# Per-head transposes straight from the loaded q and k runs, and a reordered first slot, in an attention-plus-feed-forward kernel on one Trainium2 core

## The chip, the cores and the metric

The kernel runs on one NeuronCore of one Trainium2 chip, as one launch. The metric is device time in microseconds (us); lower is better. The kernel before takes 341.52 us, the median of 4 runs (340.52 to 342.38).

## The reference

Eight batches of eight heads, 576 tokens, head size 64, everything in fp32. Each head does causal attention in a window of 128 tokens with a linear distance bias; its output, laid out as 4608 tokens by 512 features, goes through a two-layer feed-forward block.

```python
scores = scale * np.matmul(q, k.transpose(0, 1, 3, 2))
bias = slopes[:, None, None] * (-np.abs(rel).astype(np.float32))[None, :, :]
mask = (rel >= 0) & (rel < window)                      # window = 128
attn = softmax(np.where(mask, scores + bias[None], -1e9))
x = np.matmul(attn, v).transpose(0, 2, 1, 3).reshape(B * S, H * D)
h = x @ w_in                                            # 512 -> 2048
out = (h * np.clip(h + 3.0, 0.0, 6.0) / 6.0) @ w_out    # 2048 -> 512
```

## The kernel before

The attention works on pairs of heads. One pair of one batch is a step g, counted from 0 to 31: batch b = g // 4, pair hp = g % 4. Each step needs q and k with the head size on the partitions (`qTb`, `kTb`) and v with the tokens on the partitions (`vbuf`), all in bf16.

There are two ways in for q and k. Batches 0 to 2 take the first: `load_runs` puts six consecutive tokens on each of 96 partitions ("runs"), mostly by POOL's DMA queue, which casts to bf16 on the way. `prepare` (L206) copies a pair's runs into a small tile `pr`, in an order in which one [96, 128] block holds both heads of every sixth token. `transposes` (L222) turns six such blocks per tensor on PE, and `settle` (L239) copies the result from PSUM into `qTb` or `kTb`. Batches 3 to 7 take the second: `load_tokens` fetches five pieces of 128 tokens on SP's queue (L121), `cast_tokens` casts them into the single tile `tbuf` on POOL (L196), and `xbar` (L201) transposes by DMA. All loads land in four buffers, `ldbuf0` to `ldbuf3`: the runs of batches 0, 1 and 2 in `ldbuf0`, `ldbuf2` and `ldbuf0`, the first pair of batch 0 in `ldbuf3` ("wide", fp32), the token loads where `slot_of` says.

Every engine runs its instructions in the order of the program text. `first_batch` emits steps 0 to 3 and the beginning of 4, `segment` the rest. A step g emits its scores (L259 to L277), the transposes of step g + 1, the exponentials on ACT (L288, L291, L301, L309, L312), masks on POOL (`affine_select`, L294 and L304), the product with v of step g - 1 (L333, L336), the transposes of the result into `xT` (L362), `prepare(g + 2)` and then `stage_next(g)`, which issues the next loads and casts.

The feed-forward block is cut into units of four matmuls. `fill(n)` emits n units at a place in the text: an up unit `hps` (L375, followed by ACT L379 and DVE L380), or a down unit `ops` (L407). From step 9 on each step holds eight units. A finished output tile is copied to `osb` (L413, L415) and its store (L417) goes out on ACT's queue ahead of the next unit. Transfers on SP's and ACT's queues share eight completion semaphores handed round among them, so a transfer's issue also waits for the earlier transfer that used its semaphore.

Of the kernel before, what the change touches and what calls it, by code (L numbers as in the profile page):

```python
# [11 lines left out]
BF16 = mybir.dt.bfloat16  # L12
# [6 lines left out]
def kernel(  # L19
# [9 lines left out]
    nc = tc.nc  # L29
    B, H, S, D = q.shape  # L30
# [5 lines left out]
    NP = H // 2  # L36
    NQ = 5
# [3 lines left out]
    RP, RT = 96, 6  # L41
# [14 lines left out]
    ident = perm.tile([128, 128], BF16)  # L56
# [6 lines left out]
    bias_o = perm.tile([128, H], FP32)  # L63

    held = ctx.enter_context(tc.tile_pool(name="held", bufs=1))
    prs = ctx.enter_context(tc.tile_pool(name="prs", bufs=2))
    ppool = ctx.enter_context(tc.tile_pool(name="ppool", bufs=2))
    small = ctx.enter_context(tc.tile_pool(name="small", bufs=2))
    gpool = ctx.enter_context(tc.tile_pool(name="gpool", bufs=2))
# [18 lines left out]
    def slot_of(b, nm):  # L88
        if b < 3:
            return (1, 3, 1)[b]  # L90
        return (3, 1, 0, 2)[(3 * (b - 3) + "qkv".index(nm)) % 4]

    runs = {}
    for b in range(NB_PE):
        t = ldbuf[(0, 2, 0)[b]][:, :].bitcast(BF16)
        for n, nm in enumerate("qk"):
            runs[b, nm] = t[:RP, ts(n, H * RT * D)].rearrange("p (h c) -> p h c", h=H)
    wide = {nm: ldbuf[3][:RP, ts(n, 2 * RT * D)].rearrange("p (h c) -> p h c", h=2)
            for n, nm in enumerate("qk")}

    def load_runs(b, nm, hs, dst, eng):
        eng.dma_start(out=dst,
                      in_=src_of[nm][b, hs, :, :].rearrange("h (p t) d -> p h (t d)", t=RT))

    def load_pairs(b, nm, lo, hi):
        hs = slice(2 * lo, 2 * hi)
        load_runs(b, nm, hs, runs[b, nm][:, hs, :], nc.gpsimd)
# [18 lines left out]
    def constants():  # L126
        nc.vector.memset(bias3, 0.5)
        nc.vector.memset(warm, 0.0)
        nc.scalar.activation(out=warm, in_=warm, func=ACT.Exp)
        make_identity(nc, ident)  # L130
        for nm in "qk":
            load_pairs(0, nm, 1, 2)
        nc.gpsimd.iota(rel_i, pattern=[[0, 1]], base=0, channel_multiplier=1)
        base = rpool.tile([128, NT], FP32, tag="r6", name="base")
        base_i, base_b = base[:, 0:128].bitcast(INT32), base[:, 256:320].bitcast(BF16)
        nc.gpsimd.iota(base_i, pattern=[[0, 128]], base=-64, channel_multiplier=1)
        nc.gpsimd.tensor_copy(out=base_b, in_=base_i)
        nc.gpsimd.affine_select(out=base_b, in_=base_b, pattern=[[1, 128]],
                                channel_multiplier=-1, base=0,
                                compare_op=ALU.is_ge, fill=-(2.0 ** 30))  # L140
        nc.gpsimd.memset(p4buf[1], 1.0)
        nc.gpsimd.memset(kTb[1][:, :, 4, LAST:128], 0.0)
        nc.gpsimd.memset(vbuf[1][:, :, :, D:W], 1.0)
        nc.gpsimd.memset(vbuf[1][64:128, 4, :, 0:D], 0.0)
        for hp in range(2, NP):
            for nm in "qk":
                load_pairs(0, nm, hp, hp + 1)
        for nm in "qk":
            load_pairs(1, nm, 0, 2)
        nc.vector.memset(kTb[0][:, :, 4, LAST:128], 0.0)  # L150
        nc.vector.memset(vbuf[0][:, :, :, D:W], 1.0)
        nc.vector.memset(vbuf[0][64:128, 4, :, 0:D], 0.0)
        nc.vector.memset(p4buf[0], 1.0)
        for h in range(H):
            nc.vector.tensor_scalar(out=tab[:, h, :], in0=base_b, scalar1=slopes[h] / scale,
                                    scalar2=0.0, op0=ALU.mult, op1=ALU.add)
# [12 lines left out]
    def load_w_in(g):  # L169
        nc.gpsimd.dma_start(  # L170
            out=w_in_sb[:, :, ts(g, 512)],
            in_=moe_w_in[:, ts(g, 512)].rearrange("(k p) f -> p k f", p=128))
# [6 lines left out]
    def cast_v(b, j, eng):  # L179
        n = min(128, S - j * 128)  # L180
        copy = nc.scalar.copy if eng is nc.scalar else eng.tensor_copy
        copy(out=vbuf[b % 2][:n, j, :, 0:D], in_=ld[b, "v"][:n, j, :, :])
# [21 lines left out]
    st = {}  # L204

    def prepare(g):  # L206
        b, hp = divmod(g, NP)
        hs = slice(2 * hp, 2 * hp + 2)
        for nm in "qk":
            pr = prs.tile([RP, RT, 2, D], BF16, tag=f"pr{nm}", name="pr")  # L210
            if (g == 0 and nm == "k") or (nm == "q" and NP <= g < NP + 2):
                copy = nc.scalar.copy
            elif (nm == "q" and g < NP) or g == 1:
                copy = nc.vector.tensor_copy
            else:
                copy = nc.gpsimd.tensor_copy
            src = wide[nm] if g == 0 else runs[b, nm][:, hs, :]
            copy(out=pr.rearrange("p t e d -> p e t d"),  # L218
                 in_=src.rearrange("p e (t d) -> p e t d", t=RT))
            st[g, nm] = pr  # L220

    def transposes(g):  # L222
        b, hp = divmod(g, NP)
        if g > 2 * NP:
            pair = ps_sc.tile([128, 2, 512], FP32, tag="sc", name="tpp")
        tps = {}
        for nm in "qk":
            src = st.pop((g, nm)).rearrange("p t e d -> p t (e d)")
            if g > 2 * NP:
                tp = pair[:, "qk".index(nm), 0:S // 2].bitcast(BF16).rearrange(  # L230
                    "p (t a) -> p t a", t=RT)
            else:
                tp = ps_h.tile([128, RT, RP], BF16, tag="h", name="tp", padded_shape=[128, 8, 128])
            for t in range(RT):
                nc.tensor.transpose(tp[:, t, :], src[:, t, :], ident[:RP, :RP])  # L235
            tps[nm] = tp
        st[g, "tps"] = tps

# [202 lines left out]
    def stage_next(g):  # L441
        b, hp = divmod(g, NP)
        if g == 0:
            load_w_in(0)
        if g == 1:
            load_pairs(1, "q", 2, NP)
            load_pairs(1, "k", 2, NP)
        if g in (2, 3):
            load_w_in(g - 1)
        if g in (4, 5):  # L450
            load_pairs(2, "q", 2 * (g - 4), 2 * (g - 3))
            load_pairs(2, "k", 2 * (g - 4), 2 * (g - 3))
        if g == 4:
            load_w_in(3)
        if g == 5:
            load_tokens(2, "v")
        if g == 6:
            load_w_out(0)
            load_w_out(1)
            load_tokens(3, "q")  # L460
        if g in (7, 8):
            load_w_out(g - 5)
        if g == 7:
            cast_tokens(2, "v")
            load_tokens(3, "k")
        if g == 8:
            cast_tokens(3, "q")
        if g == 9:
            load_tokens(3, "v")
            xbar(3, "q")  # L470
            cast_tokens(3, "k")
        if g == 10:
            xbar(3, "k")
            load_tokens(4, "q")
        if g == 11:
            cast_tokens(3, "v")
            load_tokens(4, "k")
            load_tokens(4, "v")
            cast_tokens(4, "q")
        if b >= 3 and b + 1 < B:  # L480
            if hp < 2:
                xbar(b + 1, "qk"[hp])
            if hp in (0, 2):
                cast_tokens(b + 1, "kkv"[hp])
        if b >= 3 and b + 2 < B:
            if hp > 0:
                load_tokens(b + 2, "qkv"[hp - 1])
            if hp == 3:
                cast_tokens(b + 2, "q")
# [6 lines left out]

    def first_batch():
        transposes(0)
        settle(0)
        biases()  # L500
        prepare(1)
        for g in range(NP):
            scores(g)
            exp_diag(g, 0)
            spin(0)
            transposes(g + 1)
            settle(g + 1)
            exp_off(g, 0)
            exp_off(g, 1)
            if g == 0:  # L510
                for j in range(NQ):
                    cast_v(0, j, nc.scalar if j < 3 else nc.gpsimd)
            prepare(g + 2)
            if g == 1:
                spin(0)
            if g > 0:
                values(g - 1, (0, 1, 2))
                values(g - 1, (3, 4))
            if g > 1:
                back(g - 2)  # L520
            if g == 2:
                more_constants()
            stage_next(g)
        g = NP
        scores(g)
        back(g - 2)
        values(g - 1, (0, 1, 2))
        values(g - 1, (3, 4))
        exp_diag(g, 0)
        for j in range(3):  # L530
            cast_v(1, j, nc.gpsimd)
        exp_off(g, 0)
        exp_off(g, 1)
        transposes(g + 1)
        settle(g + 1)
        back(g - 1)
        done[0] = g
        prepare(g + 2)
        cast_v(1, 3, nc.gpsimd)
        cast_v(1, 4, nc.gpsimd)  # L540
        fill(1)
        stage_next(g)
        fill(1)

# [97 lines left out]
```

## Time and profile before

| | |
|---|---|
| median of the runs | 341.52 us (340.52 to 342.38) |
| the profiled execution's own time | 342.38 us |
| its span in the trace | 340.7 us |
| busy: PE, DVE, ACT, POOL | 316.5, 175.7, 199.0, 151.6 us |
| DMA | 48.14 MB, mean 141 GB/s over the span |
| L218 `pr` copies | 16 on POOL, 5 on DVE, 3 on ACT |
| L235 transposes | 144 of 96x96, 0.20 to 0.28 us each, pipelined |

The span is what the trace covers; 1.7 us of the execution's own time lie outside it. Busy time of PE is modelled from pipelined matmuls, so a busy PE is not one at its peak. An engine's idle time costs something only where the chain of waits passes through it. Times of day below are microseconds from the start of the span. The scores of steps 0 to 4 begin at 7.8, 12.5, 20.8, 24.4 and 27.6 us, those of step 10 at 69.0 and of step 14 at 107.4.

### The profile page before, as it was taken

To read this page: it belongs to the slowest core of one execution; us is meant where nothing else is said; L and a number is where in the kernel's file an instruction comes from. 1 tells how busy PE (TensorE), PEld (TensorE's weight loads), DVE (VectorE), ACT (ScalarE), POOL (GpSimd) and SP (SyncE) were. 2 spreads that over 40 slices of the span, in tenths; PEclk is the share of its full clock that TensorE was granted. 3 is DMA by queue.
4 is the path that set the end of the run, shared out by engine and by line. 5 is a ranking of instruction groups with operands and counts; after the bars stand their busy time and mean duration, and the time that the engine had idled before them with its cause. 6 is when DMAs were issued, how large, how long until landed. Compare 5 with 4: busy or idle time off the path is not lost.

```text
span 340.7 us, 6827 instructions
## 1 busy us (share of the span) xinstructions
PE 316.5 (93%) x2615; PEld 164.1 (48%) x2615; DVE 175.7 (52%) x362; ACT 199.0 (58%) x350; POOL 151.6 (45%) x261
## 2 busy tenths in 40 slices
PE   6488998989989999999999999999999999999995
PEld 5365655444444444545454444554455444444443
DVE  5477887646354445455545555545555444444410
ACT  3748776665457475767576757675765344343401
POOL 8389869356824763666366726632331000000000
PEclk9569999999999999999999999999999999999999
DMA  9999999999999999699959994510111000100021
GB/s 177 209 207 208 201 207 210 184 211 193 220 214 173 216 205 204 145 212 206 240 112 201 224 245 88 96 50 33 54 50 52 31 31 31 63 31 31 33 92 62
DMA packets 134831, 48.14 MB, mean 141 GB/s; under 512 B 121360, under 2 KB 130320, under 8 KB 134800
## 3 DMA queue, kind: packets, MB, share of 16 engines
q1 hardware_dynamic: 122464, 33.89, 54.8%
q0 software_dynamic: 8672, 7.44, 14.1%
q10 hardware_dynamic: 3664, 6.39, 5.4%
q8 instruction: 20, 0.33, 0.5%
q14 instruction: 11, 0.09, 0.1%
HBM read 36.70 MB, written 9.44 MB: 135 GB/s over the span
## 4 chain that ended last, share of the span: by engine, by line
PE 64%; DMA 10%; ACT 8%; DVE 6%; SPq 4%; POOL 4%; issue 4%; ACTq 0%; POOLq 0%
PE hps L375 28%; PE ops L407 27%; DMA ldbuf<-in_q_dram 5%; DMA ldbuf<-in_v_dram 4%; SPq L121 3%; DVE g L380 3%; ACT r L379 3%; ACT po L301 2%; ACT pd L291 2%; POOL pd L294 2%; DMA ldbuf<-in_k_dram 2%; PE av L336 1%; PE scd L271 1%; SPq L201 1%; PE av L333 1%
## 5 line engine op out<-in xcount | busy, mean ns | idle before, releaser
L380 DVE SCALAR_TENSOR_TENSOR g<-r,hps 128x512 bf16<-128x512 f32 x144 | 98.9, 687 | 132.0 <-ACT r L379 132.0
L379 ACT ACTIVATE r<-hps,bias 128x512 f32<-128x512 f32 x144 | 99.6, 692 | 109.2 <-PE hps L375 102.3
L375 PE MATMUL hps<-xT,w_in_sb 128*128 128x512 bf16 x576 | 146.9, 379 | 5.7 <-DVE g L380 5.5
L407 PE MATMUL ops<-w_out_sb,g 128*128 128x512 bf16 x560 | 141.8, 379 | 0.0
L407 PEld LDWEIGHTS <-g 128*128 128x128 bf16 x560 | 54.3, 98 | 63.5
L375 PEld LDWEIGHTS <-w_in_sb 128*128 128x128 bf16 x576 | 50.8, 97 | 58.7 <-issue 8.8
L304 POOL TENSOR_SCALAR_AFFINE_SELECT po<-po 128x512 bf16<-128x512 bf16 x64 | 40.1, 638 | 22.2 <-ACT po L301 19.6
L294 POOL TENSOR_SCALAR_AFFINE_SELECT pd<-pd 128x512 bf16<-128x512 bf16 x46 | 28.1, 636 | 41.0 <-ACT pd L291 41.0
L196 POOL CAST tbuf<-ldbuf 128x512 bf16<-128x512 f32 (+1 forms) x50 | 28.8, 615 | 37.2 <-issue 21.9
L301 ACT ACTIVATE po<-sco,bias_o 128x512 bf16<-128x512 f32 x64 | 43.2, 691 | 0.0
L342 DVE TENSOR_TENSOR avs<-av,rc 128x384 bf16<-128x384 f32 (+1 forms) x56 | 28.0, 500 | 1.9
L291 ACT ACTIVATE pd<-scd,bias_d 128x512 bf16<-128x512 f32 x46 | 29.0, 685 | 0.0
L336 PEld LDWEIGHTS <-pd 128*128 128x128 bf16 x256 | 19.0, 98 | 10.3 <-POOL pd L294 1.2
L333 PE MATMUL av<-vbuf,po 128*128 128x65 bf16 x224 | 21.3, 194 | 1.6 <-DVE avs L342 0.8
L336 PE MATMUL av<-vbuf,pd 128*128 128x65 bf16 x240 | 21.8, 195 | 0.6 <-POOL pd L294 0.6
L333 PEld LDWEIGHTS <-po 128*128 128x128 bf16 x256 | 19.0, 99 | 5.0 <-DVE avs L342 1.3
L413 ACT COPY osb<-ops 128x512 f32<-128x512 f32 x18 | 10.6, 586 | 12.8 <-PE ops L407 12.8
L235 PE MATMUL tp<-ident,pr 96*128 96x96 bf16 x108 | 8.4, 226 | 7.9 <-POOL pr L218 4.2
L312 ACT ACTIVATE p4buf<-sco,bias_d 128x64 bf16<-128x64 f32 x46 | 15.0, 326 | 0.0
L415 DVE COPY osb<-ops 128x512 f32<-128x512 f32 x17 | 11.6, 684 | 5.8 <-PE ops L407 5.8
L288 ACT ACTIVATE pd<-scd 128x1024 bf16<-128x1024 f32 x9 | 9.3, 1031 | 8.3 <-PE scd L271 8.3
L235 PEld LDWEIGHTS <-pr 96*128 96x128 bf16 x144 | 7.9, 105 | 12.2 <-POOL pr L218 4.4
(75 smaller groups left out, 228.0 us busy)
## 6 DMA issues: line engine op xcount, KB each, us to landing
ldbuf<-in_v_dram SPq DMA_DIRECT2D x32, 256.0 KB, 5.4
out_dram<-osb ACTq DMA_DIRECT2D x23, 256.0 KB, 3.5
ldbuf<-in_q_dram SPq DMA_DIRECT2D x20, 256.0 KB, 5.3
ldbuf<-in_k_dram SPq DMA_DIRECT2D x20, 256.0 KB, 5.5
out_dram<-osb SPq DMA_DIRECT2D x12, 256.0 KB, 2.0
w_in_sb<-in_moe_w_in_dram POOLq DMA_DIRECT2D x4, 512.0 KB, 9.0
w_out_sb<-in_moe_w_out_dram POOLq DMA_DIRECT2D x4, 512.0 KB, 8.7
ldbuf<-in_q_dram POOLq DMA_DIRECT2D x4, 288.0 KB, 8.4
```

The lines of the kernel that those rows point to most:

```text
L196: nc.gpsimd.tensor_copy(out=tbuf[:m, :, j, :], in_=s[:m, j, :, :].rearrange("p (i e) d -> p i (e d)", e=2))
L291: nc.scalar.activation(out=pd[:, e, :, :].rearrange("p j c -> p (j c)"), in_=sc[:, e, :], func=ACT.Exp, bias=bias_d[:, h:h + 1], scale=scale)
L294: nc.gpsimd.affine_select(out=pd[:, e, :, :], in_=pd[:, e, :, :], pattern=[[0, 4], [1, 128]], channel_multiplier=-1, base=0, compare_op=AL ...
L301: nc.scalar.activation(out=po[:, e, :, :].rearrange("p j c -> p (j c)"), in_=sc[:, e, :], func=ACT.Exp, bias=bias_o[:, h:h + 1], scale=scale)
L304: nc.gpsimd.affine_select(out=po[:, e, :, :], in_=po[:, e, :, :], pattern=[[0, 4], [-1, 128]], channel_multiplier=1, base=-1, compare_op=A ...
L333: nc.tensor.matmul(av[:, i, e, :], lhsT=po[:, e, qt - 1, :], rhs=vb[:, qt - 1, h, :], start=True, stop=False)
L336: nc.tensor.matmul(av[:, i, e, :], lhsT=d, rhs=vb[:, qt, h, :], start=(qt == 0), stop=True)
L342: nc.vector.tensor_tensor(out=st[g, "avs"][:, qts[0]:qts[0] + nq, :, :], in0=av[:, 0:nq, :, 0:D], in1=rc[:, 0:nq, :, :].to_broadcast([128, ...
L375: nc.tensor.matmul(hps, lhsT=w_in_sb[:, ks, ts(ms, 128)], rhs=xT[:, ks, ts(nt, NT)], start=(ks == 0), stop=(ks == n_ks - 1))
L379: nc.scalar.activation(out=r6, in_=hps, func=ACT.Relu, bias=bias3[:, 0:1], scale=1.0 / 6.0)
L380: nc.vector.scalar_tensor_tensor(out=gts[nt][:, ms, :], in0=r6, scalar=1.0, in1=hps, op0=ALU.min, op1=ALU.mult)
L407: nc.tensor.matmul(ops[nt, sub], lhsT=gts[nt][:, ms, ts(sub, 128)], rhs=w_out_sb[:, ms, :], start=(ms == 0), stop=(ms == n_ms - 1))
```

## The change

The reordering copy disappears for every step but the first. `transposes` takes the [96, 64] block of one head and one token position directly from the loaded runs and writes it to the half of the output partitions that belongs to that head, so there are twice as many transposes, each with half the columns. Step 0 still casts its fp32 runs, now in the order in which they were loaded. The pool `prs` has one buffer in place of two.

POOL issues the runs of pairs 2 and 3 of batch 0 before its memsets. The first runs of batch 1 are issued in `stage_next(0)`, ahead of the first part of w_in. The casts of batch 0's v come after `stage_next(0)` in the text. In `slot_of` two buffers change places: v of batch 3 goes to `ldbuf2` and q of batch 4 to `ldbuf0`, and so on in the same rotation.

```diff
-    prs = ctx.enter_context(tc.tile_pool(name="prs", bufs=2))
+    prs = ctx.enter_context(tc.tile_pool(name="prs", bufs=1))
...
-        return (3, 1, 0, 2)[(3 * (b - 3) + "qkv".index(nm)) % 4]
+        return (3, 1, 2, 0)[(3 * (b - 3) + "qkv".index(nm)) % 4]
...
+        for hp in range(2, NP):
+            for nm in "qk":
+                load_pairs(0, nm, hp, hp + 1)
         nc.gpsimd.memset(p4buf[1], 1.0)
         nc.gpsimd.memset(kTb[1][:, :, 4, LAST:128], 0.0)
         nc.gpsimd.memset(vbuf[1][:, :, :, D:W], 1.0)
         nc.gpsimd.memset(vbuf[1][64:128, 4, :, 0:D], 0.0)
-        for hp in range(2, NP):
-            for nm in "qk":
-                load_pairs(0, nm, hp, hp + 1)
-        for nm in "qk":
-            load_pairs(1, nm, 0, 2)
...
         for nm in "qk":
-            pr = prs.tile([RP, RT, 2, D], BF16, tag=f"pr{nm}", name="pr")
-            if (g == 0 and nm == "k") or (nm == "q" and NP <= g < NP + 2):
-                copy = nc.scalar.copy
-            elif (nm == "q" and g < NP) or g == 1:
-                copy = nc.vector.tensor_copy
-            else:
-                copy = nc.gpsimd.tensor_copy
-            src = wide[nm] if g == 0 else runs[b, nm][:, hs, :]
-            copy(out=pr.rearrange("p t e d -> p e t d"),
-                 in_=src.rearrange("p e (t d) -> p e t d", t=RT))
+            if g > 0:
+                st[g, nm] = runs[b, nm][:, hs, :]
+                continue
+            pr = prs.tile([RP, 2, RT * D], BF16, tag=f"pr{nm}", name="pr")
+            copy = nc.scalar.copy if nm == "k" else nc.vector.tensor_copy
+            copy(out=pr, in_=wide[nm])
             st[g, nm] = pr
...
-            src = st.pop((g, nm)).rearrange("p t e d -> p t (e d)")
+            src = st.pop((g, nm))
...
             for t in range(RT):
-                nc.tensor.transpose(tp[:, t, :], src[:, t, :], ident[:RP, :RP])
+                for e in range(2):
+                    nc.tensor.transpose(tp[e * D:(e + 1) * D, t, :], src[:, e, ts(t, D)],
+                                        ident[:RP, :RP])
...
         if g == 0:
+            load_pairs(1, "q", 0, 2)
+            load_pairs(1, "k", 0, 2)
             load_w_in(0)
...
-            if g == 0:
-                for j in range(NQ):
-                    cast_v(0, j, nc.scalar if j < 3 else nc.gpsimd)
             prepare(g + 2)
...
             stage_next(g)
+            if g == 0:
+                for j in range(NQ):
+                    cast_v(0, j, nc.scalar if j < 3 else nc.gpsimd)
```

## The prediction

> **What bounds the kernel now.** I read the page's slices first, then the chain of waits in order of time, then the timeline at the places where the chain leaves PE.
>
> ```profile
> PE   6488998989989999999999999999999999999995
> PEclk9569999999999999999999999999999999999999
> DMA  9999999999999999699959994510111000100021
> ```
>
> A slice is 8.5 us. From the 14th on (about 112 us) PE is full to the end: nothing there is late, and none of it is touched by the change. So the change can only move the time at which PE gets there. The DMA row is full from the start to beyond that point. That is the second resource to watch.
>
> The timeline shows the largest hole at 14 us.
>
> ```profile
> 13.50 0.61 POOL L182 CAST vbuf<-ldbuf 128x512 bf16<-128x512 f32 x1 [2.16 <-DMA ldbuf<-in_v_dram]
> 16.82 0.61 POOL L182 CAST vbuf<-ldbuf 64x512 bf16<-64x512 f32 x1 [2.71 <-DMA ldbuf<-in_v_dram]
> 17.38 0.82 POOL L218 COPY pr<-ldbuf 96x768 bf16<-96x768 bf16 x1
> ...
> 18.26 0.66 PE L235 MATMUL tp<-ident,pr 96*128 96x96 bf16 x6 [4.18 <-POOL pr L218]
> ```
>
> The bracket is the idle time before the row and what ended it. PE stands for 4.18 us for a copy that POOL could have made at 13.2 us, when the k run had landed (issued 5.96, 7.2 to landing), but POOL was held by two v casts whose pieces had not come.
>
> Between 31 and 48 us the chain goes round a loop of 6.7 us per step, on DVE as much as on PE:
>
> ```profile
> 38.31 1.90 PE hps L375 x8
> ...
> 40.96 0.69 DVE g L380
> ...
> 41.64 0.76 DVE qTb L244
> 42.40 0.66 DVE kTb L244
> ```
>
> No copy that the change removes is in this loop. Further on the chain runs through transfers:
>
> ```profile
> 65.90 5.22 DMA ldbuf<-in_k_dram
> ...
> 71.20 0.37 ACTq L417
> ...
> 71.68 0.10 ACT r L379
> ...
> 72.26 1.27 ACT pd L291 x2
> ...
> 73.57 0.67 PE tpp L235 x12
> ```
>
> The first store, on ACT's queue, is issued only when a k transfer of batch 3 has landed at 71.1: it reads no k, but shares its completion semaphore. ACT stood 1.96 us, and PE then 0.93 us for `pd`. The same happens at 91.6 us with a q transfer, and the last such place is here:
>
> ```profile
> 98.54 4.57 SPq L201
> ...
> 103.15 3.94 DMA ldbuf<-in_v_dram
> ...
> 109.39 1.18 POOL pd L294 x2
> ...
> 111.80 0.20 PE av L333
> ```
>
> POOL had waited 9.7 us for a DMA transpose, and PE found its mask just in time at 111.8.
>
> **What the Trainium skill says.** "TensorEngine Tiling", Performance Considerations: stationary operands of at most 64 columns can be packed two abreast; Restrictions: column tiling switches Fast Weight Load off. No row of this trace has 64 stationary columns; the nearest, the scores on half the rows, come at 28 ns each (8 in 0.39 us, the last 0.20), against 60 ns for the blocks of 128 columns in L362 (5 in 0.44). "TensorE: Matmul & The Clock Gate", Part 3: weight loads overlap running matmuls only for different row groups; the two heads here share theirs. Its section LDWEIGHTS prices a load at columns / 1.2 ns, 53 ns for 64. "DMA: Bandwidth & Descriptors", Queues, rings and completion order: all queues take turns on the same 16 engines. The trace agrees: while POOL's queue is full a 256 KB piece on SP's takes 13 to 22 us to land, against a median of 5.4.
>
> **The change, part by part.**
>
> *Copies.* POOL loses 16 x 0.821 = 13.1 us, DVE four (3.1 us with one of 1.50), ACT two (1.7 us). On the path are those of the first 28 us; afterwards POOL's idle time covers them (1.6 to 2.5 us before its masks at 42.8 and 49.5), and DVE and ACT lose none after step 5. The two casts of step 0 stay; a plain order instead of a permuted one I take at zero (0.72 and 0.83 us now, at best half).
>
> *The hole.* Transposes(2) can start at 13.4 and be settled at about 15.0. The product of step 0 then needs the last v piece, landed at 16.6 now. With 0.59 MB of batch 1 out of the queue, at about 210 GB/s, it lands 2.8 us sooner; POOL, after masks until 11.35 and three DMA issues of 0.68 to 0.76 us, is at the casts at 13.5 and done by 14.7. Scores(2) at 15.2 instead of 20.8; if v lands as now, 17.5.
>
> *Batch 1's first runs.* Issued at 7.8 and 8.5 now, 11.4 and 12.1 after, so k lands at 12.1 plus 9.4 (a later pair's time; bounds 8.0 and 11.8) = 21.5. The k transposes of step 4, at 25.3 now, wait for that: of 5.6 us gained **3.8** remain (1.4 to 5.2). w_in, issued 5 us sooner, is needed at 31. The four POOL memsets slip 2.5 us behind four DMA issues; p4buf's first reader is at 15.2. prs with one buffer is used once: nothing.
>
> *Twice the transposes.* 144 more, all before 75 us. The spacing now is (0.67 - 0.206)/11 = 42 ns. Call the new one s. Two abreast would be 23 ns, one after the other 42, bound by the weight load 53, load and matmul in turn 95. I take **53**. In the loop of steps 4 to 7, DVE wants q at 41.64, 0.46 us after the transposes begin: q is late by 12s - 0.26 = 0.38 us, k by less. Four times makes 1.5. Steps 9 and 10 add 24s - 0.51 = 0.76 us on PE each, 1.5. So 3.0 of the 3.8 go, and PE comes **0.8 us early** to the store at 70 us. With 23 or 42 ns it is 3 to 4 us early.
>
> *Slots.* The runs in ldbuf2 are last read by transposes(7), near 42 us, v comes at 72; those in ldbuf0 by transposes(11), 74.2, q at 82.9. SP's queue holds k and v of batch 4 behind that load, so a slip beyond 8 us would delay them; none is in sight. Nothing.
>
> *The queue.* Here I decide. When the k transfer lands is a matter of the bytes before it: v of three batches, three batches of runs, both weights, q of batch 3, some 13 MB at about 200 GB/s. None goes away; they only change order. POOL's transfers go out 3 to 4 us sooner, take turns with SP's as before and end sooner; the k transfer ends where the sum ends. What can be won is a dip:
>
> ```profile
> 16.00:18.00 2.00, 0.00 (x0) 0.00 (x0) 0.00 (x0) 0.00 (x0) 1.18 (x2) 0.50 1.27 234
> 18.00:20.00 2.00, 1.74 (x25) 1.60 (x26) 1.04 (x2) 0.00 (x0) 1.99 (x4) 0.50 0.83 180
> ```
>
> (The two last columns are DMA share and GB/s.) With w_in and the runs queued by then it fills: 2 x (1.25 - 0.83)/1.25 = **0.7 us**. Bounds: 0, as the pieces may only be reordered, and 2 us if the dips at 37 and 60 us fill too. After 72 us the SP chain (transposes through the single `tbuf`, L201) keeps its own pace, so 0.7 us is what reaches 111.8.
>
> Sum: 342.38 - 0.7 = 341.7 for the profiled execution, which lies 0.86 above the median; against the median 341.52 - 0.7 = **340.8 us**.
>
> **Rivals.** Half a percent, 1.7 us, is about what a measurement can tell here.
>
> *A: the queue takes it back* (above). For it: the chain enters transfers three times between 51 and 112 us, ACT already waits at the store. Against: the DMA row is not quite full near 60 and 75 us. 339.8 to 342.2. Also here: the early part doing nothing at all, since any gain is dropped at the store.
>
> *B: the head's gain goes through.* Then the k transfer was late because its predecessors were issued late, not because the wires were full. Speaks for it: SP issued one q piece at 51.4 that landed 11.4 us later, and single issues took up to 6 us. With 23 or 42 ns a transpose worth 2.5 to 4 us: 337.5 to 339.0.
>
> *C: slower.* The place is the loop and steps 9 and 10: heads share row groups, so each weight load waits for the transpose before it, s = 95 ns. Then k is late by 24s + 0.16 - 1.14 = 1.3 us in each of four steps, and steps 9 and 10 pay 1.77 each: 8.7 us against 3.8 gained and 1.9 of ACT's slack, 3.0 us late. 344.5. It decides from s = 74 ns on, where 144s - 4.9 = 5.7. For it: the skill's two sentences on weight loads. Against: loads of 128 columns hide behind 42 ns now.
>
> **How the numbers follow.** A 0.44, B 0.31, C 0.25. The predicted time is A's, 340.8. The tails of A across 339.8 are put against those of B across it, so faster 0.32, same 0.43, slower 0.25. The range leaves out the best of B and the worst of C: 337.8 to 344.5.
>
> **What would show it.** L218 left with two rows, POOL's busy time near 138 us. PE's wait at 14 us under 1 us and PEclk's third slice above 6. A PE wait for `ldbuf` at 19 to 22 us. 288 transposes; their spacing gives s directly. The store's ACT wait longer than 1.96 us and its k transfer landing near 70.5: A. That landing at 68 or before: B. No ACT wait at the store, and steps 4 to 7 longer than 6.7 us: C. Scores of step 14 at 106.7 for A, 104 for B, 110 for C. Wrong altogether if the time changes and the stretch after 112 us is not shifted as a whole.

## The result, and the profile after

The changed kernel takes **344.44 us** (median of 32 runs, 342.28 to 346.0), the kernel before 341.91 us in the same comparison (53 runs). The ratio is 1.0079, 95% interval [1.0062, 1.0095]: slower by 0.8%. Ratios here and below leave out runs more than 1.5% above the fastest of their kernel. The profiled execution of after took 344.55 us (span 342.8), that of before 342.38 (340.7).

The page of after, busy tenths per slice and the granted clock (a slice is now 8.6 us):

```profile
PE   6398799999969999999999999999999999999995
PEclk9969899999999999999999999999999999999999
DMA  9999899999995999599949996310111000100021
```

The PE row is still full from the 14th slice on, so the loss is ahead of that. There are two new marks: the 12th PE slice (94 to 103 us) falls from 8 to 6, and in the fifth (34 to 43 us) PE falls from 9 to 7 and the clock to 8.

The timeline of after around the first hole (start, busy us, engine, line, what, and in brackets the idle time before it and what ended it):

```profile
11.21 0.70 PE L230 MATMUL tp<-ident,ldbuf 96*64 96x96 bf16 x24
...
16.34 0.61 POOL L180 CAST vbuf<-ldbuf 128x512 bf16<-128x512 f32 x1 [3.23 <-DMA ldbuf<-in_v_dram]
...
17.00 0.21 PE L332 MATMUL avh<-vbuf,pd 128*128 128x65 bf16 x1 [2.83 <-POOL vbuf L180]
...
17.38 0.61 POOL L180 CAST vbuf<-ldbuf 64x512 bf16<-64x512 f32 x1 [0.43 <-DMA ldbuf<-in_v_dram]
```

The first row settles the price of the new transposes: 24 end within 0.70 us, of which the last alone takes some 0.2, so they follow one another at (0.70 - 0.206) / 23 = 21 ns on average. In the trace the starts come in pairs, 3 to 4 ns apart within a pair and some 43 ns from pair to pair: the two heads of one token position run side by side. Twice as many cost hardly more than the 12 of before (0.67 us). The rows below show that the hole moved rather than closed: PE no longer waits for a copy but for v itself.

Step 5, where the loop of 31 to 48 us had run undisturbed before:

```profile
35.57 1.17 POOL L180 CAST vbuf<-ldbuf 128x512 bf16<-128x512 f32 x2 [4.32 <-DMA ldbuf<-in_v_dram]
...
36.24 0.21 PE L332 MATMUL avh<-vbuf,pd 128*128 128x65 bf16 x1 [2.18 <-POOL vbuf L180]
...
36.93 3.17 PE L371 MATMUL hps<-xT,w_in_sb 128*128 128x512 bf16 x8
```

In before neither the cast nor the product waits there:

```profile
33.89 1.17 POOL L182 CAST vbuf<-ldbuf 128x512 bf16<-128x512 f32 x2
...
35.54 0.20 PE L333 MATMUL avh<-vbuf,po 128*128 128x65 bf16 x1
```

v of batch 1 is late in after: its last two pieces land at 35.5 and 35.9 us, against 29.2 and 30.3 before. PE stands for 2.18 us, and the matmuls after the wait then come every 427 ns instead of 213.

The third store, first in before, then in after:

```profile
91.67 0.34 ACTq L417 DMA_DIRECT2D out_dram<-osb  x1
...
92.11 0.69 ACT L379 ACTIVATE r<-hps,bias 128x512 f32<-128x512 f32 x1 [2.45 <-PE av L336]
...
94.27 0.20 PE L333 MATMUL av<-vbuf,po 128*128 128x65 bf16 x1 [0.81 <-DVE avs L342]
```

```profile
95.30 0.34 ACTq L413 DMA_DIRECT2D out_dram<-osb  x1
...
95.75 0.69 ACT L375 ACTIVATE r<-hps,bias 128x512 f32<-128x512 f32 x1 [3.95 <-DMA ldbuf<-in_k_dram]
...
97.91 0.20 PE L329 MATMUL av<-vbuf,po 128*128 128x65 bf16 x1 [2.32 <-DVE avs L338]
```

`osb` was ready at 91.8 in after, but the store went out only at 95.3, when a k piece of batch 4 had landed (95.2). The store does not read k; it shares that piece's completion semaphore. In the traces the first three stores of before signal semaphores 102, 102 and 118, those of after 104, 104 and 102. In before the third store waits for a q piece that lands at 91.6. The loads on SP's queue are the same and come in the same order in both traces, so why the deal changed isn't shown. order_only (below) has the deal of before and straight_only that of after: it came with the transposes, the missing copies or the exchanged buffers, not with the moved loads.

The starts of the scores give the balance along the program: before against after, +/- is after minus before, each figure rounded by itself.

| scores of step | before | after | difference | what happened in between |
|---|---|---|---|---|
| 2 | 20.8 | 19.3 | -1.6 | copy gone, v late |
| 5 | 33.9 | 32.1 | -1.8 | |
| 6 | 40.6 | 43.0 | +2.4 | v of batch 1 |
| 10 | 69.0 | 72.0 | +3.0 | |
| 11 | 79.8 | 82.0 | +2.1 | before waits at the first store, after comes too late to wait |
| 13 | 99.3 | 102.9 | +3.6 | third store |
| 15 | 117.5 | 119.1 | +1.6 | before waits for POOL's mask behind the `tbuf` cast, after comes too late to wait |
| 31 | 251.2 | 252.8 | +1.6 | |

Two losses (4.2 and 1.5 us), and 0.6 us in steps 6 to 9, thus stand against one gain and two waits that before has and after has not. Each trace is one execution. The start of step 5 lies between 33.9 and 34.9 us in the four traces below that share the first steps of before, and between 31.1 and 32.5 in those that share them with after, so differences of about 1 us there say nothing. The last 0.5 us of the 2.1 between the spans comes after the scores of step 31 and was not followed up.

### The profile page after: what moved, and what is told of

Its sections match the earlier page's. It is cut to its first block, busy times and chain, and to the rows that moved or that the text cites. A ratio compares the mean times of both kernels' runs of the same rounds, so it can differ in the third digit from the quotient of the medians.

```text
span 342.8 us, 7083 instructions
## 1 busy us (share of the span) xinstructions
PE 317.6 (93%) x2759; PEld 164.6 (48%) x2759; DVE 172.3 (50%) x358; ACT 197.9 (58%) x348; POOL 139.3 (41%) x245
## 4 chain that ended last, share of the span: by engine, by line
PE 71%; DMA 10%; ACT 7%; DVE 5%; SPq 3%; issue 2%; POOL 2%; ACTq 0%
PE hps L371 32%; PE ops L403 30%; DMA ldbuf<-in_v_dram 8%; DVE g L376 3%; ACT r L375 3%; SPq L121 3%; DMA ldbuf<-in_k_dram 2%; PE av L332 2%; ACT po L297 2%; PE scd L267 2%; POOL pd L290 1%; PE av L329 1%; PE sco L273 1%; PE ops L387 1%; ACT pd L287 1%
## 5 line engine op out<-in xcount | busy, mean ns | idle before, releaser
L375 ACT ACTIVATE r<-hps,bias 128x512 f32<-128x512 f32 x144 | 99.6, 692 | 112.6 <-PE hps L371 106.6
L329 PEld LDWEIGHTS <-po 128*128 128x128 bf16 x256 | 19.3, 99 | 13.7 <-issue 8.0
L332 PE MATMUL av<-vbuf,pd 128*128 128x65 bf16 x240 | 21.5, 195 | 1.7 <-ACT vbuf L180 1.7
L267 PE MATMUL scd<-qTb,kTb 64*128 64x128 bf16 x256 | 12.6, 219 | 0.0
L187 POOL CAST vbuf<-ldbuf 128x1024 bf16<-128x1024 f32 x12 | 12.2, 1045 | 0.0
```

The lines of the kernel that those rows point to most:

```text
L329: nc.tensor.matmul(av[:, i, e, :], lhsT=po[:, e, qt - 1, :], rhs=vb[:, qt - 1, h, :], start=True, stop=False)
L332: nc.tensor.matmul(av[:, i, e, :], lhsT=d, rhs=vb[:, qt, h, :], start=(qt == 0), stop=True)
L375: nc.scalar.activation(out=r6, in_=hps, func=ACT.Relu, bias=bias3[:, 0:1], scale=1.0 / 6.0)
```

## The experiments

Theory S: the third store's semaphore makes the difference. Theory V: the late v of batch 1 makes it. Later came K, the clock; G, gates whose times are set by DMAs; and H and N, whether the change has a worth behind these gates. Each run was compared with runs of the kernel before on the same chip; medians of before were 341.3 to 342.0 us.

### The parts apart, and each suspect taken away

order_only is the kernel before with the reordering alone (the moved loads and v casts). straight_only is the changed kernel with loads and casts in the old order; the change in `slot_of` stays in it. w_in_later is the changed kernel with

```diff
@@ stage_next
         if g == 0:
             load_pairs(1, "q", 0, 2)
             load_pairs(1, "k", 0, 2)
-            load_w_in(0)
         if g == 1:
             load_pairs(1, "q", 2, NP)
             load_pairs(1, "k", 2, NP)
+            load_w_in(0)
```

and stores_pool the changed kernel with

```diff
             eng = nc.sync if done[0] == G else nc.scalar
+            if nt * 4 + sub < 4:
+                eng = nc.gpsimd
```

> The kernel before with only the reordering of the change: pairs 2 and 3 of batch 0 issued ahead of the memsets, batch 1's first runs and w_in in slot 0, batch 0's v cast last; copies, transposes and buffers as before. Theory S (the third store, which after the change shares its semaphore with a k piece that lands at 95 us instead of a q piece that lands at 92): the third store still waits for the q piece here, so 341.5 to 342.5 us, about the kernel before. Theory V (v of batch 1, pushed from 30 to 36 us by transfers pulled ahead of it, decides): v lands at 34 us or later, PE waits some 2 us at step 5, and the time is 343.5 to 344.5 us, like the changed kernel.

> The changed kernel with the load and cast order of the kernel before: only the per-head transposes, the missing copies and the two exchanged buffers are left. Theory S: the third store waits for the k piece at 95 us as in the changed kernel, whatever PE gained before, so scores of step 13 at about 103 us and 343.5 to 344.5 us. Theory V: v of batch 1 lands at 30 us as before, no wait at step 5, 340.5 to 342 us.

> The changed kernel with the first part of w_in issued one slot later, behind batch 1's second runs. Theory V: batch 1's v lands some 4 us sooner than 36 us, the wait at step 5 (2.2 us) shrinks to under 1 us and the time falls by 1.5 to 2.5 us, to about 342. Theory S: the wait at step 5 shrinks too, but PE then stands longer at the third store, which still goes at 95 us: 343.5 to 344.5 us.

> The changed kernel with its first four stores issued on POOL's queue in place of ACT's, so that ACT never waits for the semaphore of another transfer. Theory S: ACT's wait of 4.0 us at 95 us is gone, scores of step 13 at 100 to 101 instead of 102.9, and the time falls by 1.5 to 3 us, to 341.5 to 343. Theory V: PE is 2 to 3 us late from step 6 on whatever the store does; 344 to 344.5 us.

| | median us | ratio to before |
|---|---|---|
| order_only | 342.40 | 1.0024 [1.0004, 1.0045] |
| straight_only | 343.64 | 1.0071 [1.0045, 1.0098] |
| w_in_later | 344.48 | 1.0092 [1.0066, 1.0118] |
| stores_pool | 342.70 | 1.0038 [1.0018, 1.0059] |

V as the decider falls. In w_in_later the pieces land at 26.5 and 29.9 us, PE has no wait at step 5 and reaches step 6 1.6 us ahead of before, and the time is no better. S gets support: all four medians lie in its ranges, straight_only's too, and without waits on stores half the loss is gone, although v is as late as in after.

S's sign for straight_only, scores of step 13 at about 103 us, is not in the trace, which has 99.8. But that execution took 341.45 us, 2.2 less than the median (w_in_later's took 342.44, 2.0 less). The third store has after's semaphore in both, and its k piece came early, at 92.1 and 93.1 us. In the three profiled executions with that deal that took 344.3 to 344.7 us (after, later_spin and straight_two_act) it landed between 94.3 and 95.2, and scores of step 13 began at 102.6 to 103.0. So the third store probably costs the usual execution of straight_only its 0.7% too; no trace shows one.

The trace shows another loss, at the first store. PE reaches step 10 1.5 us early, and then the step takes 13.2 us instead of 10.8. Timeline of straight_only, with its third store at the end:

```profile
70.64 0.37 ACTq L415 DMA_DIRECT2D out_dram<-osb  x1
...
71.12 0.69 ACT L377 ACTIVATE r<-hps,bias 128x512 f32<-128x512 f32 x1 [2.94 <-PE hps L373]
...
73.01 0.83 PE L232 MATMUL tpp<-ident,ldbuf 96*64 96x96 bf16 x24 [1.90 <-ACT pd L289]
...
73.77 1.89 PE L405 MATMUL ops<-w_out_sb,g 128*128 128x512 bf16 x4
...
92.21 0.34 ACTq L415 DMA_DIRECT2D out_dram<-osb  x1
...
92.65 0.69 ACT L377 ACTIVATE r<-hps,bias 128x512 f32<-128x512 f32 x1 [2.10 <-PE av L334]
```

The first store goes out when the last k piece of batch 3 has landed at 70.6; PE, having come early, stands 1.90 us, and the four matmuls after it take 1.89 us instead of 1.03. The table of stretches of the same kernel (us, busy time and count of PE, PEld, DVE, ACT and POOL, then PEclk, DMA share, GB/s):

```profile
74.00:76.00 2.00, 2.00 (x13) 1.00 (x12) 0.26 (x1) 1.11 (x4) 2.00 (x5) 0.50 1.05 235
76.00:78.00 2.00, 2.00 (x14) 0.97 (x12) 1.83 (x4) 0.56 (x1) 2.00 (x4) 0.79 0.75 163
```

The granted clock is at half for some 3.4 us. In step 10 an early PE is therefore worse than a punctual one: it makes a hole long enough to lose the clock, and 1.5 us ahead of before turn into 0.9 us behind.

### Is it the clock, and is it the stores?

later_spin tests the first question by adding work in the hole. It is w_in_later with

```diff
-        for ks in range(n_ks):
+        for ks in list(range(n_ks)) * times[0]:    # 3 in the third fill of step 10
             nc.tensor.matmul(hps, ...
```

The other three put the first four stores on POOL's queue, as in stores_pool: later_pool in w_in_later, straight_pool in straight_only, before_pool in the kernel before.

> The changed kernel with w_in(0) issued after batch 1's second runs (w_in_later, 344.5 us), and the up matmuls of the unit ahead of the hole of step 10 run three times over, which gives the same values: 8 more 512-column matmuls, 1.7 us of TensorE at full clock, in a place where the profile of w_in_later shows TensorE idle for 2.65 us (71.6 to 74.25) because ACT waits with the first store. After that hole the 512-column matmuls of w_in_later are spaced 427 ns instead of 213 for 3.5 us. Theory K (the clock: a hole of about 2 us in TensorE's work is followed by some 3.4 us at half clock, which costs 1.7 us on top of the hole): the spacing stays 213 ns, scores of step 11 start at about 80.5 instead of 82.2, and the time falls by 1.7 us to about 342.8 although there is more work. Theory S (only what the stores wait for counts): the extra work hides in the hole and the time stays at 344.5, or it comes on top, 345 to 346.

> w_in_later with its first four stores on POOL's queue, so neither v of batch 1 is late nor does ACT wait with a store. Both S and K: no hole at steps 5, 10 and 12 and no half clock after 23 us; steps 10 to 11 and 12 to 13 take about 10 us each, and 3 to 5 us of the 344.5 go: 339.5 to 341.5, at or below the kernel before. If the stores are not what takes the head's gain back, about 343 to 344.

> The kernel before with the per-head transposes alone (straight_only, 343.6 us), first four stores on POOL's queue. S and K: the 3.0 us ACT wait at step 10, the 1.9 us hole and the half clock after it go, and the late third store: 339 to 341 us. If the per-head transposes cost time by themselves (serialized weight loads), it stays at 343 or above.

> The kernel before, first four stores on POOL's queue. Its own first store waits 2.0 us on ACT and makes a hole of 0.93 us in TensorE's work; the third comes with no wait. S and K: 0.5 to 1.5 us less than before, 340 to 341 us, so what POOL's queue brings later_pool and straight_pool beyond that is what the change brought on. If POOL's masks suffer from the four more issues: 341.5 to 342.5.

| | median us | ratio to before |
|---|---|---|
| later_spin | 344.70 | 1.0111 [1.0074, 1.0148] |
| later_pool | 343.63 | 1.0077 [1.0050, 1.0104] |
| straight_pool | 342.58 | 1.0017 [0.9987, 1.0047] |
| before_pool | 340.95 | 0.9992 [0.9957, 1.0028] |

later_spin did at its place what K says: the hole is 1.25 instead of 2.65 us, the clock stays full, and step 10 takes 13.0 instead of 14.2 us with 1.7 us more work in it. The time did not follow; it is S's 344.5, not K's 342.8. The third store's k piece lands at 94.4, step 12 takes 12.7 us (9.1 where nothing waits, 9.5 in the trace of w_in_later), and the clock drops there, at 98 us, instead.

before_pool lies in its range of 340 to 341, though its ratio shows no gain. later_pool is well above what both theories expected (it lies in the 343 to 344 noted for the case that the stores are not what takes the gain back), and straight_pool somewhat. With these stores off ACT, steps 10 and 12 take 9.9 and 9.1 us, as they should. Step 11 takes 10.3 in straight_pool, where a cast into `tbuf` and then a store hold up POOL's masks until 78.6. It still reaches step 14 2.4 us ahead of before. Then that step takes 12.9 us instead of 8.1. The timeline of straight_pool there:

```profile
104.70 2.84 POOL L196 CAST tbuf<-ldbuf 128x512 bf16<-128x512 f32 x5 [8.24 <-DMA qTb<-tbuf]
107.49 0.55 POOL L417 DMA_DIRECT2D out_dram<-osb  x1
108.05 1.23 POOL L292 TENSOR_SCALAR_AFFINE_SELECT pd<-pd 128x512 bf16<-128x512 bf16 x2
...
108.75 0.20 PE L334 MATMUL av<-vbuf,pd 128*128 128x65 bf16 x1 [1.32 <-POOL pd L292]
```

There is one `tbuf`. POOL may not put k of batch 4 in it until the DMA transpose of q has read it and landed, at 104.6; until then POOL stands, and the masks queue behind the cast. PE waits for masks from 107 on, and at half clock from 110.5 to 113.9. later_pool has the same (12.5 us).

That gave theory G: up to about 115 us the DMA stream sets three times before which PE can't pass, the first store near 71, the third at 92 to 95 and POOL's cast near 105. What PE gains ahead of one of them it loses there, with the clock on top. The stream itself moves little: over all 20 traces the last k piece of batch 3 lands between 70.1 and 73.7 us, and the third v piece of batch 4 between 99.6 and 103.1, whether PE is early or late.

### The gates opened

The first three stores go to POOL's queue, and k gets a staging buffer of its own (its room comes from `prs`, whose two tiles for step 0 move into `qTb` of batch 1):

```diff
-    tbuf = held.tile([128, NP, NQ, 128], BF16, name="tbuf")
+    tbufs = {nm: held.tile([128, NP, NQ, 128], BF16, name=f"tbuf{nm}") for nm in "qk"}
...
-            pr = prs.tile([RP, 2, RT * D], BF16, tag=f"pr{nm}", name="pr")
+            pr = qTb[1].rearrange("p h j c -> p (h j c)")[
+                :RP, ts("qk".index(nm), 2 * RT * D)].rearrange("p (e x) -> p e x", e=2)
...
+            if nt * 4 + sub < 3:
+                eng = nc.gpsimd
```

This is straight_two, on straight_only; later_two is the same on w_in_later, after_two on the changed kernel; straight_two_act has the second buffer alone.

> straight_only (the kernel before with the per-head transposes) with its first three stores on POOL's queue and two staging buffers tbuf, one for q and one for k (the first pair's bf16 runs go into qTb of batch 1, for room), so that the cast of k doesn't wait on POOL until the DMA transpose of q has landed, and POOL's masks don't wait behind it. In straight_pool TensorE reaches step 14 2.4 us ahead of before (105.0) and then needs 12.9 us for it, the last 3.5 us at half clock. Theory G (the head's gain is held back at gates set by DMAs: the first store at 71, the third at 92, POOL's cast at 105): with all three gates gone, step 14 takes about 8.1 us, step 15 starts at 113 instead of 117.9, and the time is 337.5 to 339.5, less than before. Theory S (only the stores' waits take time): like straight_pool, 341.5 to 343.

> The same two edits (first three stores on POOL's queue, two buffers tbuf) in the changed kernel with w_in(0) issued after batch 1's second runs (later_pool, 343.6 us). Theory G: 338.5 to 340.5. Theory S: about 343.6 as later_pool.

> The same two edits in the changed kernel with nothing else moved, so v of batch 1 stays late at step 5 (scores of step 6 at 43, 2.5 us behind before). Theory G: TensorE comes to the gates late and finds them open anyway, so the second buffer brings nothing beyond stores_pool (342.7): 341.5 to 343. Theory V (the late v decides once the gates are gone): 2 to 3.5 us above later_two.

> straight_only with the two buffers tbuf alone, stores on ACT's queue as before. Theory G: the gates of the first and third store stay: scores of step 11 at 80 to 81 with a hole and half clock ahead of them; step 14 is no gate there because TensorE is late: 342.5 to 344, like straight_only's 343.6. If POOL's cast alone is what counts: 339 to 340.

| | median us | ratio to before |
|---|---|---|
| straight_two | **337.63** | 0.9880 [0.9850, 0.9910] |
| later_two | 338.52 | 0.9913 [0.9882, 0.9944] |
| after_two | 341.39 | 0.9988 [0.9967, 1.0010] |
| straight_two_act | 343.87 | 1.0044 [1.0018, 1.0069] |

Three times lie in G's ranges, and after_two's is 0.1 us below its own. Two details went otherwise. In straight_two_act PE came to step 10 later than in straight_only and lost little there; the loss is at the third store, where step 12 takes 13.4 us, although PE comes to it 0.2 us later than before does: its k piece lands at 94.3. So being early is not all; this store's other partner costs time by itself. And after_two is below stores_pool, so the second buffer did bring something there: in stores_pool step 18 takes 9.0 us behind a cast into `tbuf`, in after_two 8.1. The timeline of straight_two at the place of the last fence:

```profile
96.78 2.28 POOL L197 CAST tbufk<-ldbuf 128x512 bf16<-128x512 f32 x4
99.49 0.61 POOL L197 CAST tbufk<-ldbuf 64x512 bf16<-64x512 f32 x1 [0.43 <-DMA ldbuf<-in_k_dram]
...
107.99 1.23 POOL L294 TENSOR_SCALAR_AFFINE_SELECT pd<-pd 128x512 bf16<-128x512 bf16 x2 [4.32 <-ACT pd L291]
```

The cast is done at 100.1, as soon as k is there, and the mask now waits for ACT instead of the other way round. Steps 10, 12 and 14 take 9.9, 9.1 and 8.1 us, and PE is 4.4 us ahead of before from step 15 to the end. The second buffer alone brings straight_only nothing that can be measured, since the stores stop PE first. Once the gates are open the late v of batch 1 counts in full: after_two, which differs from later_two only in when w_in is issued, is 2.9 us above it. straight_two beats both kernels. One gate is left: in step 9, 10.7 instead of 9.9 us, PE stands 0.55 us for a transfer of w_out (0.88 in later_two).

### Has the change a worth of its own, and what is the third store's part?

The kernel before has no room for a second buffer of the same kind. So the cast of batch 4's k was first moved one step later on POOL, behind the masks (before_gates, straight_gates, after_gates, each with three stores on POOL's queue):

```diff
         if b >= 3 and b + 1 < B:
+            if g == 13:
+                cast_tokens(4, "k")
             if hp < 2:
                 xbar(b + 1, "qk"[hp])
-            if hp in (0, 2):
+            if hp == 2 or (hp == 0 and b > 3):
                 cast_tokens(b + 1, "kkv"[hp])
```

after_third is the changed kernel with its third store alone on POOL's queue (`nt * 4 + sub == 2`).

> The kernel before with its first three stores on POOL's queue and POOL's cast of batch 4's k moved one step later, behind the masks of step 13 and ahead of its own DMA transpose. It loses 0.9 us at step 10 (hole at 73.6) and 2.0 us in step 14 (10.1 instead of 8.1 us). Theory H (the head's gain is real and only held back): before gains about 2 to 3 us, 339 to 340, and stays 2 us above straight_gates. Theory N (the change's head gain is nothing; the gates are all there was): before_gates equals straight_gates within 0.5 us, both near 338.

> straight_only with the same edits as before_gates. H and N: 337.5 to 339, like straight_two. If the later cast of k makes its DMA transpose late for step 16 (due at 125, now landing near 122), it is 1 to 2 us more.

> The changed kernel with the same edits as before_gates. v of batch 1 stays late at step 5 (2.2 us hole and 3.4 us at half clock). H: 341 to 342, like after_two, so 2.5 to 3.5 us above straight_gates; N: the same, since both have the late v.

> The changed kernel with its third store alone on POOL's queue. Theory S3 (the third store's wait of 4.0 us on ACT and the 2.3 us hole behind it are what sets after apart from before): step 12 takes 9 to 10 us instead of 11.8, and the time is 342 to 343, like stores_pool's 342.7. If POOL's cast in step 14 becomes the gate instead (POOL issues the third store, and TensorE is 2 us earlier there): 343.5 to 344.5.

| | median us | ratio to before |
|---|---|---|
| before_gates | 342.95 | 0.9977 [0.9948, 1.0005] |
| straight_gates | 344.54 | 1.0086 [1.0050, 1.0122] |
| after_gates | 343.12 | 1.0048 [1.0029, 1.0067] |
| after_third | 342.37 | 1.0010 [0.9982, 1.0039] |

after_third answers its question: step 12 takes 9.1 us, and the 0.8% is gone. Of the changed kernel's loss against before, that one wait is all that can be measured. (stores_pool has this edit too and keeps 0.4%; its trace loses 0.9 us at step 18 and 0.8 us between steps 20 and 24.)

The other three lie above the ranges of both theories and leave H and N open, because they ran into the next gate. straight_gates is 5.3 us ahead of before at step 15, and then step 18 takes 15.0 us: the single `tbuf` again, now with batch 5 (the q transpose lands at 139.3, POOL's cast of k runs from 139.45 to 142.3, and the masks come after it). before_gates' 22 runs scatter from 338.0 to 346.5 us, half of them above 343, so no one figure stands for it.

So the second buffer was laid where the reorder copies of the first three batches had been, which are dead by then, in the kernel before (before_two) and in order_only (order_two):

```diff
-    tbuf = held.tile([128, NP, NQ, 128], BF16, name="tbuf")
+    room = held.tile([128, 4 * 2 * RT * D], BF16, name="room")
+    tbufs = {"q": held.tile([128, NP, NQ, 128], BF16, name="tbufq"),
+             "k": room[:, 0:NP * NQ * 128].rearrange("p (h j c) -> p h j c", h=NP, j=NQ)}
...
-            pr = prs.tile([RP, RT, 2, D], BF16, tag=f"pr{nm}", name="pr")
+            pr = room[:RP, ts(2 * (g % 2) + "qk".index(nm), 2 * RT * D)].rearrange(
+                "p (t e d) -> p t e d", t=RT, e=2)
```

> The kernel before with straight_two's edits: first three stores on POOL's queue, a second staging buffer for k, which for want of room lies where the reorder copies of the first three batches were (POOL's cast of batch 3's k waits for the last of them, at step 10). Theory H (the head's gain of the per-head transposes is real, 1.5 to 2 us, and was only held back): 339 to 340.5, that is 1.5 to 3 us above straight_two's 337.6. Theory N (the gates were all there was): 337 to 338.5.

> order_only with the edits of before_two. v of batch 1 is late at step 5 as in order_only and after_two (hole and half clock, scores of step 6 about 2.5 us behind before): 341 to 343, 1.5 to 3 us above before_two in theory H and in theory N, since the late v is a gate that these edits don't open; if it comes out at before_two, the late v is made up later.

| gates | neither part | transposes alone | reordering alone | both |
|---|---|---|---|---|
| as they are | 1 | 1.0071 [1.0045, 1.0098] | 1.0024 [1.0004, 1.0045] | 1.0079 [1.0062, 1.0095] |
| open | 0.9891 [0.9856, 0.9926] | 0.9880 [0.9850, 0.9910] | 0.9968 [0.9953, 0.9983] | 0.9988 [0.9967, 1.0010] |

The transposes' columns include the two exchanged buffers. before_two takes 338.50 us, at the upper end of N's range, and order_two 340.68, just under the range it was given. N holds as far as these runs can tell: with the gates open the kernel before is as fast as straight_two, within the intervals. A gain of the per-head transposes of a few tenths of a per cent is not excluded: from step 15 on straight_two's trace is 1.1 us ahead of before_two's, in spite of its wait for w_out, which before_two has not. The reordering costs 0.8 to 1.1% (0.9968 against 0.9891, 0.9988 against 0.9880), by the late v of batch 1. With the gates as they are it is the other way round: the late v costs little, because PE comes to the gates late. The transposes alone cost 0.7%, and it goes when the gates are opened. How much of it is PE's early coming and how much the third store's other semaphore was not taken apart.

## Why the prediction was wrong

The step that decided was that the 0.7 us won at 18 us "is what reaches 111.8", that is, that the stores and casts downstream wait as in before. The third store waited instead for a k piece that landed at 95.2, not for the q piece at 91.6; step 12 grew from 10.3 to 11.8 us. With that store on another queue the kernel is level with before (1.0010). The steps of the prediction one by one:

**Twice the transposes: mis-sized.** I took 53 ns and charged 3.0 us. They come at 21 ns, a little under the low end. Steps 5 to 10 are each 0.13 to 0.17 us longer than in before_two where nothing waits (straight_pool), 0.9 us together; what sets that was not followed up. "TensorEngine Tiling", Performance Considerations, was right that 64 stationary columns pack two abreast, as the pairs of starts 3 to 4 ns apart show; the weight-load sentences that I held against it did not bind, since a pair with both its loads took 43 ns. So rival C's mechanism is refuted, although its 344.5 us is what was measured.

**The hole: half right.** The copy's wait is gone, but scores(2) start at 19.3, not 15.2. The step that failed is "it lands 2.8 us sooner": the last v piece of batch 0 landed at 17.3, later than the 16.8 of before. Moving batch 1's runs back made room for batch 0's own runs, issued 1.3 us earlier, and for w_in soon after; the transfers that take turns with v were exchanged, not removed.

**Batch 1's first runs: mis-sized on the safe side.** They landed at 17.9 and 20.0, not 21.5, so they held nothing up. The gain is 1.8 us at step 5 instead of 3.8, because the hole stayed.

**The DMA order: the step with the wrong sign.** I wrote that w_in, "issued 5 us sooner, is needed at 31", and that POOL's transfers "take turns with SP's as before". I asked who waits for the moved transfers, not whom they hold up. It was v of batch 1 on SP's queue, whose last pieces came 5.6 and 6.3 us later: a 2.18 us hole plus about 1.7 us for the half clock after it, which is 3.9 of the 4.2 us between steps 5 and 6. w_in_later shows the cause; the wait disappears with w_in put back. In before the five pieces took 9.6 to 11.3 us from issue to landing (my "13 to 22 us" held only for later ones), in after 12.4 to 15.6. PE thus came to step 10 3.0 us late, not 0.8 us early at the store; two waits that before has and after has not gave 2.9 us back later.

**The gates: right in kind, incomplete in number.** Case A said that a gain is dropped at the first store, since the k transfer's time is a matter of the bytes ahead of it. That held in the traces of straight_only and w_in_later. In after itself it did not show, because PE arrived late: the k piece landed at 72.8, just as the store was ready, and the ACT wait that was to be longer than 1.96 us is 0.94. From there on I let 0.7 us pass to the end. I had shown the 91.6 us store and the single `tbuf` at 103 to 112 and yet costed both as unchanged. I did not think that the store's partner could change, although the semaphores are handed round: an edit of the program can deal them anew. The third store cost 3.95 us on ACT, and after_third shows that it accounts for the measured loss.

**What I had no term for** is the clock. A hole was worth its own length in all my sums. "TensorE: Matmul & The Clock Gate", Part 1, says that activity is judged in a free-running window of 3.4 us and that an idle one halves the rate. On the length the traces agree: drops lasted 3.41 us, or 6.83 us (two windows), as in order_only after holes of 1.62 and 1.17 us. In after's clock record the rate changes at 15.64, 22.47, 36.12 and 39.53 us, which are 2, 4 and 1 windows apart, and the other traces keep such a grid too. The page's section "Why this matters for your kernels" advises against gaps of more than about 3 us; here the measurement decides, and that is too mild: holes of 1.90, 2.18, 2.50 and 2.65 us all lost the clock. One of 2.32 us (after, 97.9) did not. Counted on that grid over all traces, from 22 us to 4 us before the end, 15 windows at full rate had PE busy for less than half, and 14 of them were followed by half rate. The exception is this one, 42% busy, and one window at 60% (after_third) was also followed by a drop. So a window need not be idle to cost the clock, and the exact limit stays open.

**Rival B** would have needed open gates. straight_two at 337.63 us lies in its 337.5 to 339.0, but the kernel before gets there as well, so it is the gates, as far as the intervals tell, and not the head that were worth the 1%.

**Right as foretold:** two rows of the reorder copy left, 288 transposes, POOL busy for 139.3 us, the stretch after 119 us shifted as a whole by 1.6 us, no wait for a buffer in sight from the exchanged slots, although no run takes those alone and they may have dealt the semaphores anew. Not as foretold: PE waited 1.7 and 2.8 us for v in the first hole, the clock's third slice stayed at 6, and scores of step 14 began at 111.0, near the 110 of rival C, by another way.

## What to carry to other kernels

Before a stage is made faster, list the waits downstream whose end is set by something else (a transfer's landing, a single staging buffer, a shared semaphore) and ask how early the faster engine may come to each: ahead of them a gain is worth nothing, or less than nothing once the hole is long enough to lose the clock. For a transfer moved forward, ask who takes turns with it, not only who reads it. And keep stores off an engine that the critical path needs, because a store's semaphore partner can change with an edit that leaves the transfers of its queue as they were.

## What the runs showed of the hardware that I had not expected

- Transposes with 64 stationary columns, both heads on the same rows and side by side in the columns, start in pairs 3 to 4 ns apart, a pair every 43 ns (after, 11.2 us): two cost what one of 128 columns cost (42 ns).
- TensorE idle for 1.9 us can be followed by 3.41 us at half clock, which about doubles the hole's price. The changes of rate lie on one grid of 3.41 us in each trace, and what counts is nearer to the busy share of a window than to the hole's length: 14 of 15 windows under half busy were followed by a drop.
- The store that waits for a shared semaphore holds ACT up: ACT stood 2.0 us (before, first store) to 4.9 us (straight_two_act, third store) for a transfer that the store has nothing to do with.
